# RWKV-7 recurrence and a squared-ReLU feed-forward on one core: the first product for two chunks at a time, the second in whole tiles

## The chip, the core and the metric

One core of a Trainium2 chip. The metric is the device time of one execution in microseconds. PE is TensorE with its matmuls (PEld its weight loads), DVE is VectorE, ACT is ScalarE, POOL is GpSimd, SP is SyncE, whose queue issues the loads and stores.

## What is computed

```python
def _attn_ref(r, k, v, w, a, b):        # each (4, 8, 768, 40), float32
    state = np.zeros((B, H, D, D))
    for t in range(S):
        y[:, :, t] = einsum('bhd,bhde->bhe', r_t, state)
        Sa = einsum('bhde,bhe->bhd', state, a_t)
        state = state * w_t[:, :, None, :] - Sa (x) b_t + v_t (x) k_t
    return y

def _moe_ref(x, w_in, w_out):           # x: 3072 x 320, w_in: 320 x 2048, w_out: 2048 x 320
    g = np.maximum(x @ w_in, 0.0) ** 2
    return g @ w_out

# x is y with the heads of a token side by side
```

## The kernel before

The sequence of 768 steps is cut into 12 chunks of 64 tokens. A chunk holds 64 tokens of 4 batches, 256 tokens in all. For each chunk c the work is:

- `load`: SP issues the loads of w, k, b, a, v, r (`ldw` ... `ldr`), 320 KB each, into buffers that alternate between two chunks.
- `prep`: ln of w (ACT), its split into two bf16 parts `hi` and `lo`, cumulative sums by matmuls (`ci`, `cx`, `cg`), their exponentials (`ei`, `ex`, `eg` on ACT), the scaled k and b (`mulKB`), a (`mulA`), and casts of r and v; transposes on PE (`TK`, `TA`) with their evictions (`tK`, `tA`, `tR`).
- `rec`: the masked products `EN` (masked by `mEN` on DVE, line 542), then `AS`, `EV`, `u0`, `NU`, `u1`, and the state `S`, `SC`, `s`, `TS`, `tS`. This goes from chunk to chunk.
- `read`: `TV`, `CX` (masked by `mCX`, line 542), `RS`, `Y`, `y`, `yd`, and the transposes `XT`, evicted by `xt` into the tile XT: the feed-forward's input, transposed.
- `ffn`: four operations `F c u0` to `F c u3` multiply XT by a quarter of w_in each into a PSUM slot; `f` (ACT, line 747) is the relu into the tile G, `q` squares G in place (DVE, line 753, or POOL, line 755); four operations `O c u0` to `O c u3` multiply G by w_out into one PSUM slot, `o` evicts it, `st` stores it.

PE's array is used in halves. F, the transposes, EN, CX and `ci` run as two half-arrays of 64 rows by 128 columns (mode "R"); O, EV, NU, S, Y, AS, RS, `cx`, `cg` as two of 128 rows by 64 columns (mode "C"). Consecutive matmuls alternate between the halves. One F is 20 matmuls with 256 columns each, one O is 16 with 320. There are four PSUM slots, each of 2 x 512 float32 a partition.

All operations are recorded in a `Plan` with their predecessors, but the order in which they are issued, the engine of each and the PSUM slot of each are written out by hand in the string ORDER, as entries "engine (slot) name". `Plan.issue` follows it: each engine gets its instructions in this order, and each waits for what it reads. Numbers such as `FETCH`, `SWITCH` or the durations in `plan.add` are notes from which such an order was made; at run time they do nothing. A helper records the matmuls (line 356 for products, 360 for transposes), so the lines of the profile name helpers and the tiles tell which operation it is.

An excerpt of ORDER, where PE's second form follows the first:

```
PE0 F 1 u0; POOL hi 4; ACT f 1 u3; DVE mulA 3; POOL wout1; PE1 F 0 u2; DVE lo 4; ACT f 1 u0;
DVE mulKB 3 h0; PE2 CX 2 g0; POOL mulKB 3 h1; PE3 CX 2 g1; ACT f 0 u2; PE0 F 1 u2
```

Of the kernel before, what the change touches and what calls it, by code (L numbers as in the profile page):

```python
# [23 lines left out]
class Plan:  # L24
# [6 lines left out]
    LINE, FETCH = 256, 3500  # L31
# [62 lines left out]
AS 1; DVE mEN 1 g1; PE1 TS 0; PE2 CX 0 g1; ACT tS 0; POOL win1; DVE mCX 0 g1; PE EV 1; SP ldv 2;
PE0 CX 0 g0; ACT u0 1 g1; DVE mCX 0 g0; ACT u0 1 g0; POOL mulKB 2 h1; PE NU 1; DVE mulKB 2 h0; PE1
Y 0; ACT u1 1 g0; PE2 TK 2; DVE y 0; ACT u1 1 g1; SP ldw 3; DVE mulA 2; ACT tK 2; PE0 TV 1; POOL
castR 2; PE1 S 1; DVE yd 0; POOL win0; PE SC 1; DVE tV 1; SP lda 3; PE3 XT 0; PE2 TA 2; ACT xt 0;
DVE s 1 q1; PE0 CX 1 g0; ACT tR 2 g1; DVE s 1 q0; PE3 F 0 u3; ACT tA 2; DVE mCX 1 g0; PE1 TS 1;
POOL castV 2; ACT tR 2 g0; DVE tS 1; PE0 CX 1 g1; ACT f 0 u3; PE2 F 0 u1; SP ldw 4; DVE mCX 1 g1;
ACT ln 3; PE1 EN 2 g0; PE3 EN 2 g1; ACT f 0 u1; POOL hi 3; DVE mEN 2 g0; PE0 RS 1; PE Y 1; SP ldb  # L100
3; POOL lo 3; PE2 AS 2; DVE mEN 2 g1; PE1 F 0 u0; DVE y 1; POOL win2; SP ldk 3; PE EV 2; ACT f 0
u0; PE3 cx 3; DVE yd 1; DVE u0 2 g1; PE0 ci 3 h1; ACT u0 2 g0; PE cg 3; POOL q 0 u1; ACT ei 3 h1;
PE NU 2; ACT eg 3; PE1 ci 3 h0; DVE u1 2 g0; ACT u1 2 g1; PE0 XT 1; ACT ln 4; DVE xt 1; PE2 S 2;
POOL q 0 u0; PE SC 2; ACT ei 3 h0; SP ldr 3; PE0 TV 2; DVE s 2 q0; ACT ex 3; PE1 F 1 u1; DVE tV 2;
POOL wout0; PE3 F 1 u3; ACT f 1 u1; DVE s 2 q1; PE0 F 1 u0; POOL hi 4; ACT f 1 u3; DVE mulA 3;
POOL wout1; PE1 F 0 u2; DVE lo 4; ACT f 1 u0; DVE mulKB 3 h0; PE2 CX 2 g0; POOL mulKB 3 h1; PE3 CX
2 g1; ACT f 0 u2; PE0 F 1 u2; DVE mCX 2 g1; PE1 cx 4; ACT f 1 u2; POOL castR 3; DVE mCX 2 g0; PE
cg 4; POOL wout2; SP ldr 5; PE3 TK 3; ACT ex 4; PE0 ci 4 h0; POOL q 0 u2; DVE tK 3; PE2 TA 3; ACT
eg 4; PE1 RS 2; ACT tR 3 g0; PE Y 2; DVE tA 3; SP ldv 3; ACT tR 3 g1; PE3 O 0 u0; POOL wout3; ACT
ei 4 h0; DVE y 2; SP ldw 5; PE2 EN 3 g0; DVE yd 2; PE O 0 u1; DVE mEN 3 g0; PE0 EN 3 g1; POOL q 1  # L110
u0; PE1 ci 4 h1; DVE mEN 3 g1; PE2 XT 2; ACT ei 4 h1; PE O 0 u2; DVE q 1 u1; POOL q 0 u3; PE1 AS
3; PE0 O 1 u0; SP ldk 4; DVE zu 3; ACT castV 3; DVE q 1 u2; PE O 1 u1; DVE q 1 u3; ACT xt 2; SP
ldb 4; PE EV 3; PE O 1 u2; DVE u0 3 g1; ACT u0 3 g0; PE O 0 u3; PE NU 3; DVE o 0; ACT ln 5; PE O 1
u3; ACT u1 3 g1; DVE u1 3 g0; POOL hi 5; SP st 0; PE2 TS 2; SP lda 4; ACT o 1; POOL zu 4; DVE lo
5; PE3 TV 3; ACT tS 2; PE1 F 2 u1; SP ldr 4; DVE tV 3; POOL castR 5; PE0 F 2 u0; ACT f 2 u1; DVE
mulKB 4 h0; PE2 CX 3 g0; SP ldk 5; PE3 F 2 u3; ACT f 2 u0; POOL q 2 u1; DVE mCX 3 g0; SP lda 5;
PE1 CX 3 g1; PE0 ci 5 h0; ACT f 2 u3; DVE mulKB 4 h1; PE2 F 2 u2; POOL q 2 u0; DVE mCX 3 g1; ACT
ei 5 h0; SP ldb 5; PE3 cx 5; ACT f 2 u2; PE0 RS 3; DVE q 2 u3; PE cg 5; POOL castR 4; PE Y 3; ACT
ex 5; DVE mulA 4; PE1 ci 5 h1; POOL q 2 u2; SP ldv 4; PE2 TK 4; ACT eg 5; DVE y 3; ACT ei 5 h1;
PE3 TA 4; PE1 S 3; DVE tK 4; ACT tA 4; PE SC 3; POOL yd 3; SP ldw 6; PE0 O 2 u0; ACT tR 4 g0; DVE  # L120
s 3 q0; POOL mulA 5; ACT tR 4 g1; PE2 EN 4 g1; PE O 2 u1; DVE mEN 4 g1; SP ldr 6; PE3 XT 3; DVE s
3 q1; POOL mulKB 5 h0; PE2 EN 4 g0; ACT xt 3; PE O 2 u2; DVE mulKB 5 h1; SP st 1; DVE mEN 4 g0;
PE1 TA 5; POOL castV 4; PE3 TK 5; ACT tR 5 g0; PE O 2 u3; DVE tK 5; ACT tR 5 g1; PE2 AS 4; ACT o
2; PE EV 4; DVE tA 5; PE3 TS 3; ACT u0 4 g0; SP st 2; DVE u0 4 g1; PE0 F 3 u1; SP ldw 7; ACT ln 6;
DVE tS 3; SP ldv 5; POOL hi 6; PE NU 4; ACT f 3 u1; PE1 EN 5 g0; DVE u1 4 g0; PE3 F 3 u0; POOL lo
6; SP ldr 7; DVE u1 4 g1; PE0 F 3 u3; ACT f 3 u0; DVE mEN 5 g0; POOL zu 5; SP ldk 6; PE2 ci 6 h1;
ACT f 3 u3; PE3 TV 4; POOL q 3 u0; PE1 S 4; SP ldb 6; DVE tV 4; ACT ei 6 h1; PE SC 4; PE0 cx 6; PE
cg 6; DVE s 4 q0; POOL q 3 u1; PE2 CX 4 g0; ACT ex 6; SP ldb 7; PE3 F 3 u2; DVE s 4 q1; ACT eg 6;
ACT castR 6; DVE mCX 4 g0; PE0 EN 5 g1; PE1 O 3 u0; ACT f 3 u2; SP lda 6; DVE mEN 5 g1; ACT castV
5; POOL q 3 u2; PE2 CX 4 g1; PE3 ci 6 h0; PE O 3 u1; DVE q 3 u3; ACT ei 6 h0; SP ldw 8; DVE mCX 4  # L130
g1; PE0 AS 5; ACT ln 7; PE3 RS 4; PE O 3 u2; POOL hi 7; DVE mulKB 6 h0; PE Y 4; POOL lo 7; PE EV
5; DVE y 4; PE O 3 u3; ACT u0 5 g0; DVE u0 5 g1; POOL yd 4; ACT o 3; DVE mulKB 6 h1; PE NU 5; POOL
mulA 6; PE2 ci 7 h0; SP st 3; ACT u1 5 g0; DVE u1 5 g1; PE3 XT 4; PE1 TK 6; SP ldr 8; ACT ei 7 h0;
DVE xt 4; PE0 TS 4; SP lda 7; ACT tK 6; POOL zu 6; PE2 TV 5; DVE tS 4; SP ldv 6; PE3 F 4 u0; DVE
tV 5; POOL castR 7; PE0 TA 6; ACT f 4 u0; SP ldk 7; PE1 F 4 u1; DVE tR 6 g0; ACT tR 6 g1; POOL q 4
u0; DVE tA 6; PE2 CX 5 g1; PE3 F 4 u2; ACT f 4 u1; DVE mCX 5 g1; SP ldv 7; PE0 EN 6 g0; PE1 F 4
u3; ACT f 4 u2; POOL q 4 u1; DVE mEN 6 g0; PE2 CX 5 g0; SP ldw 9; ACT f 4 u3; PE3 S 5; DVE mCX 5
g0; PE SC 5; POOL castV 6; PE0 EN 6 g1; ACT ln 8; PE1 ci 7 h1; DVE mEN 6 g1; PE2 O 4 u0; ACT ei 7
h1; SP ldb 8; POOL q 4 u2; DVE s 5 q1; PE1 RS 5; PE0 cx 7; PE cg 7; DVE s 5 q0; PE Y 5; ACT ex 7;
DVE mulKB 7 h1; PE3 AS 6; POOL hi 8; PE EV 6; ACT castR 8; DVE mulA 7; PE O 4 u1; POOL zu 7; ACT  # L140
u0 6 g0; DVE y 5; PE O 4 u2; ACT eg 7; ACT u0 6 g1; POOL q 4 u3; DVE mulKB 7 h0; PE NU 6; DVE yd
# [700 lines left out]
```

## Time and profile before

| | us |
|---|---|
| median of 3 runs | 269.33 (268.33 to 271.39) |
| the profiled execution, time | 270.12 |
| its span, first to last instruction | 268.4 |
| PE busy in it | 226.9 (85%) |
| DVE busy | 198.1 (74%) |
| ACT busy | 160.1 (60%) |
| POOL busy | 141.5 (53%) |

The granted TensorE clock was 0.975 of full speed on average. Busy time of an engine is the union of its instructions. In the profile's groups a line reads: line, engine, operation, out<-in with shapes, count, then busy time and mean ns of one, then the idle time of the engine just before them and what ended it. "issue" as releaser means that the engine waited for nothing the profile shows. The queues of part 3 are those of the DMA engines; q8 carries instructions.

### The profile page before, as it was taken

How to read it: one execution, taken by the hardware profiler on the slowest of the kernel's cores; microseconds unless marked ns; L12 is line 12 of the kernel's file. 1: busy time of each engine (PE TensorE's matmuls, PEld its weight loads, DVE VectorE, ACT ScalarE, POOL GpSimd, SP SyncE). 2: the span in 40 equal slices, each digit the busy share in tenths (PEclk: the TensorE clock that was granted, in tenths of full speed). 3: DMA queues.
4: the chain of work that ended last, by engine and by line, in shares of the span. 5: the costliest groups of instructions: out<-in, count | busy, mean ns of one | idle time of the engine just before them, and what ended most of it. 6: DMA issues, size and time to landing. Idle time of an engine off the chain costs nothing.

```text
span 268.4 us, 14323 instructions
## 1 busy us (share of the span) xinstructions
PE 226.9 (85%) x6712; PEld 193.6 (72%) x6712; DVE 198.1 (74%) x219; ACT 160.1 (60%) x201; POOL 141.5 (53%) x119
## 2 busy tenths in 40 slices
PE   0557884987979998997998898997879999999992
PEld 0335774776869986876888786886767888878881
DVE  7456578495886797996789898894888697867620
ACT  3346565636735774674674784775756877674631
POOL 4384634086570686674599287793483293232020
PEclk9999999597999999999799999999999999999999
DMA  7999999975993579799898298799980410200213
GB/s 116 185 185 143 153 193 149 136 127 58 171 171 56 114 142 142 180 169 153 181 155 116 53 145 155 133 124 171 158 165 8 89 19 2 54 5 2 51 26 74
DMA packets 135995, 31.06 MB, mean 116 GB/s; under 512 B 125185, under 2 KB 135937, under 8 KB 135937
## 3 DMA queue, kind: packets, MB, share of 16 engines
q1 hardware_dynamic: 131136, 27.53, 62.8%
q0 software_dynamic: 4800, 2.62, 7.7%
q8 instruction: 52, 0.85, 1.4%
q14 instruction: 7, 0.05, 0.1%
HBM read 28.84 MB, written 3.93 MB: 122 GB/s over the span
## 4 chain that ended last, share of the span: by engine, by line
PE 63%; DVE 13%; issue 7%; ACT 5%; DMA 5%; SPq 4%; POOL 3%; ACTq 0%; POOLq 0%; DVEq 0%
PE pb L356 55%; PE pb L360 8%; DMA raw_kb<-in_k_dram 2%; DVE KB L352 2%; DMA raw_r<-in_r_dram 2%; POOL lo L350 1%; ACT VU L342 1%; DVE EN L542 1%; DVE Yb L337 1%; DVE VU L339 1%; SPq L385 1%; SPq L778 1%; POOL tR L346 1%; DVE Yb L702 1%; ACT VUT L342 1%
## 5 line engine op out<-in xcount | busy, mean ns | idle before, releaser
L755 POOL TENSOR_TENSOR G<-G 128x1024 bf16<-128x1024 bf16 x30 | 57.6, 1929 | 53.0 <-ACT G L747 52.6
L356 PE MATMUL pb<-WOUT,G 128*64 128x320 bf16 x768 | 59.4, 300 | 3.8 <-issue 3.7
L747 ACT ACTIVATE G<-pb 128x1024 bf16<-128x1024 f32 x48 | 49.0, 1024 | 22.2 <-PE pb L356 21.1
L356 PE MATMUL pb<-XT,WIN 64*128 64x256 bf16 x960 | 60.8, 273 | 1.0 <-issue 0.9
L356 PEld LDWEIGHTS <-WIN 64*128 64x128 bf16 x960 | 46.9, 96 | 6.4 <-issue 1.7
L356 PEld LDWEIGHTS <-G 128*64 128x64 bf16 x768 | 42.9, 110 | 11.4 <-issue 5.5
L542 DVE TENSOR_TENSOR EN<-pb,MSK 128x1024 bf16<-128x1024 f32 x24 | 29.1, 1221 | 6.3 <-PE pb L356 6.0
L542 DVE TENSOR_TENSOR CX<-pb,MSK 128x1024 bf16<-128x1024 f32 x24 | 29.0, 1218 | 4.4 <-PE pb L356 4.2
L346 POOL CAST hi<-lnW 128x640 bf16<-128x640 f32 x11 | 8.6, 779 | 37.1 <-ACT lnW L409 17.9
L431 ACT ACTIVATE iG<-pb 128x640 f32<-128x640 f32 x24 | 16.8, 702 | 11.3 <-PE pb L356 10.6
L352 DVE TENSOR_TENSOR KB<-raw_kb,iG 128x640 bf16<-128x640 f32 x17 | 18.8, 1113 | 6.2 <-ACT iG L431 3.7
L356 PEld LDWEIGHTS <-EN 128*64 128x64 bf16 x768 | 16.4, 118 | 7.4 <-issue 5.3
L342 ACT ACTIVATE NZ<-pb 64x640 bf16<-64x640 f32 x19 | 13.2, 697 | 13.6 <-PE pb L356 9.0
L634 DVE TENSOR_TENSOR STb<-pb,gL 64x640 bf16<-64x640 f32 x22 | 18.1, 821 | 4.2 <-PE pb L356 3.7
L342 ACT ACTIVATE AR<-pb 128x512 bf16<-128x512 bf16 (+1 forms) x24 | 15.5, 667 | 8.3 <-PE pb L360 5.4
L753 DVE TENSOR_TENSOR G<-G 128x1024 bf16<-128x1024 bf16 x18 | 17.5, 979 | 3.0 <-ACT G L747 3.0
L342 ACT ACTIVATE VU<-pb 64x640 bf16<-64x640 f32 x15 | 10.5, 698 | 9.8 <-PE pb L356 7.3
L339 DVE TENSOR_SCALAR VU<-pb 64x640 bf16<-64x640 f32 x9 | 7.4, 823 | 10.0 <-ACT VU L342 6.2
L350 POOL TENSOR_TENSOR KB<-raw_kb,iG 128x640 bf16<-128x640 f32 x7 | 11.4, 1628 | 5.8 <-DMA raw_kb<-in_k_dram 3.6
L356 PE MATMUL pb<-hi,UTI 64*128 64x320 bf16 x48 | 8.6, 342 | 7.0 <-POOL hi L346 6.9
L342 ACT ACTIVATE osb<-pb 128x640 f32<-128x640 f32 x11 | 7.8, 705 | 11.2 <-PE pb L356 11.1
L350 POOL TENSOR_TENSOR lo<-lnW,hi 128x640 bf16<-128x640 f32 x8 | 13.0, 1622 | 2.4 <-PE pb L360 2.0
(88 smaller groups left out, 454.3 us busy)
## 6 DMA issues: line engine op xcount, KB each, us to landing
raw_w<-in_w_dram SPq DMA_DIRECT2D x24, 160.0 KB, 5.0
raw_kb<-in_k_dram SPq DMA_DIRECT2D x12, 320.0 KB, 6.1
raw_r<-in_r_dram SPq DMA_DIRECT2D x24, 160.0 KB, 4.1
raw_kb<-in_b_dram SPq DMA_DIRECT2D x12, 320.0 KB, 6.7
raw_a<-in_a_dram SPq DMA_DIRECT2D x24, 160.0 KB, 5.2
raw_v<-in_v_dram SPq DMA_DIRECT2D x12, 320.0 KB, 6.6
out_dram<-osb SPq DMA_DIRECT2D x24, 160.0 KB, 2.7
WIN<-in_moe_w_in_dram POOLq DMA_DIRECT2D x8, 160.0 KB, 4.6
```

Source lines behind the costliest of these rows:

```text
L342: alts.append(("ACT", c_act(n), lambda: nc.scalar.activation(out=o_(), in_=i_(), func=ACTF.Copy, scale=1.0 if scale is None else scale)))
L346: lambda: nc.gpsimd.tensor_copy(out=o_(), in_=i_())))
L350: return [("POOL", 130 + 2.35 * n, lambda: nc.gpsimd.tensor_tensor(out=o_(), in0=a_(), in1=b_(), op=op)), ("DVE", c_dve(n), lambda: nc.vec ...
L352: ("DVE", c_dve(n), lambda: nc.vector.tensor_tensor(out=o_(), in0=a_(), in1=b_(), op=op))]
L356: return lambda: nc.tensor.matmul(out=o_(), lhsT=l_(), rhs=r_(), start=start, stop=stop, skip_group_check=True)
L360: return lambda: nc.tensor.transpose(out=o_(), in_=i_(), identity=IDb[rows(g), :])
L431: ew(f"ei {c} h{jh}", [("ACT", c_act(2 * n), lambda hb=hb, jh=jh: nc.scalar.activation(out=iG[0][:].rearrange("p (g j) e -> p g (j e)", g= ...
L542: evac(f"m{nm} {c} g{g}", lambda s, n: [("DVE", c_dve(n), lambda: nc.vector.tensor_tensor(out=dst[q2][:, g, s].rearrange("p q i t -> p (q ...
L634: ew(f"s {c} q{q}", [("DVE", c_dve(2 * n), lambda q=q: nc.vector.tensor_tensor(out=STb[q2][rows(q), :, q, 0:D], in0=slot(hs, FP32)[rows(q) ...
L747: ("ACT", c_act(1024), lambda gb=gb, hf=hf: nc.scalar.activation(out=gb, in_=slot(hf, FP32)[:], func=ACTF.Relu)),
L753: ("DVE", 165 + 0.7 * 1024, lambda gv=gv: nc.vector.tensor_tensor(out=gv, in0=gv, in1=gv, op=ALU.mult)),
L755: ("POOL", 1900, lambda gv=gv: nc.gpsimd.tensor_tensor(out=gv, in0=gv, in1=gv, op=ALU.mult))],
```

## The change

Chunks are put in groups: chunk 0 alone, then pairs (1, 2) to (9, 10), chunk 11 alone. For a group of two, F runs with 512 columns, both chunks side by side in XT; one F operation then covers one block of 128 columns of w_in in each half (`v0`, `v1`) and fills the same PSUM slot, with 10 matmuls. O stays per chunk, but in whole tiles: 128 rows by 128 columns (mode "D"), 8 matmuls instead of 16 an operation. G holds a whole group and there is one of it instead of two for a chunk each. The two buffers of v lie in the lower and upper 64 partitions of one tile. ORDER is a new one: the same 911 entries in number, in another sequence and with other choices of engine (f three times on DVE; q 24 times on each of DVE and POOL instead of 18 and 30; mulKB 13 times on POOL instead of 7). Its notes on load and fetch durations are changed too.

```diff
-    LINE, FETCH = 256, 3500
+    LINE, FETCH = 256, 4350
...
+GROUPS = ((0,), (1, 2), (3, 4), (5, 6), (7, 8), (9, 10), (11,))
+NGB = 1
-ORDER = """SP ldw 0; SP ldk 0; SP ldw 1; SP ldr 0; ACT ln 0; POOL hi 0; SP ldb 0; POOL zu 2; DVE lo 0; SP lda
+ORDER = """DVE zu 0; SP ldw 0; SP lda 0; SP ldr 0; SP ldb 0; ACT ln 0; SP ldw 1; POOL hi 0; POOL zu 1; SP ldk
+0; POOL lo 0; ACT castR 0; PE0 cx 0; PE1 ci 0 h0; SP ldr 1; PE2 ci 0 h1; PE cg 0; SP ldv 0; ACT ln
...
+AS 5; PE EV 5; DVE tA 6; PE3 F 4 u0v0; DVE tR 6 g0; ACT u0 5 g0; DVE u0 5 g1; PE0 F 4 u3v1; SP ldk
+7; ACT f 4 u0v0; DVE mulKB 6 h1; POOL mulKB 6 h0; PE NU 5; DVE f 4 u3v1; PE3 cx 7; ACT u1 5 g1; PE
+cg 7; POOL q 4 u0v0; SP ldw 8; ACT ei 7 h0; DVE u1 5 g0; PE0 TK 6; ACT ex 7; PE1 ci 7 h1; DVE tK
...
+g0; PE2 F 4 u3v0; DVE tS 4; POOL q 4 u1v1; DVE mCX 5 g0; PE0 TS 5; SP lda 7; ACT f 4 u3v0; PE3 F 4
+u1v0; DVE tS 5; SP ldw 9; POOL q 4 u0v1; ACT ln 8; PE1 EN 6 g1; PE2 CX 5 g1; ACT f 4 u1v0; PE0 F 4
+u2v1; DVE mEN 6 g1; PE3 TK 7; POOL hi 8; DVE mCX 5 g1; ACT f 4 u2v1; PE1 AS 6; PE EV 6; POOL lo 8;
+ACT castR 7; DVE tK 7; PE0 O 3 u0; ACT u0 6 g0; SP ldr 9; POOL q 4 u2v1; DVE q 4 u1v0; PE2 ci 8
...
-    raw_v = buf("raw_v", [64, NH, D], FP32, NV)
+    raw_v = buf("raw_v", [128, NH, D], FP32)[0]
...
-    XT = buf("XT", [128, NKB, NT], BF16, 2)
-    G = buf("G", [128, NFB, NT], BF16, 2)
+    XT = buf("XT", [128, NKB, 2 * NT], BF16, 2)
+    G = buf("G", [128, NFB, 2 * NT], BF16, NGB)
...
-                 nc.sync.dma_start(out=raw_v[c % NV][:], in_=whole(v))}),
+                 nc.sync.dma_start(out=raw_v[rows(c % NV)], in_=whole(v))}),
...
+    def up(gi):
+
+        gr = GROUPS[gi]
+        c, w = gr[-1], NT * len(gr)
+        gb = G[gi % NGB]
+        xt = XT[gi % 2]
+        per = 512 // w
+        for u in range(4):
+            for v_ in range(2 // per):
+                hf = ("F", c, u, v_)
+                us = f"u{u}" + (f"v{v_}" if per == 1 else "")
+                blk = range(v_ * per, v_ * per + per)
+                ms = []
+                for i in blk:
+                    for kb_ in range(NKB):
+                        for rg in range(2):
+                            ms.append(mm(
+                                lambda rg=rg, i=i, hf=hf: slot(hf, FP32)[
+                                    :, rg, w * (i % per):w * (i % per) + w],
+                                lambda rg=rg, kb_=kb_, i=i, u=u: WIN[
+                                    rows(rg), kb_, 256 * u + 128 * i:256 * u + 128 * i + 128],
+                                lambda rg=rg, kb_=kb_: xt[rows(rg), kb_, 0:w],
+                                i == blk[0] and kb_ == 0, kb_ == NKB - 1))
+                pe(f"F {c} {us}", "R", w, ms,
+                   reads=[("XT", gi % 2, ci) for ci in range(len(gr))] + [("WIN", u)],
+                   writes=[hf], alloc=[hf])
...
+        for c in gr:
+            down(c, gi, gr.index(c))
+
+    def down(c, gi, ci):
...
             for j in range(4 * u, 4 * u + 4):
                 for g in range(2):
-                    for bb in range(2):
-                        ms.append(mm(
-                            lambda g=g, bb=bb: slot(ho, FP32)[rows(bb), g, 0:DM],
-                            lambda g=g, bb=bb, j=j: G[q2][
-                                :, j, (2 * g + bb) * L:(2 * g + bb) * L + L],
-                            lambda j=j: WOUT[:, j, :], j == 0, j == NFB - 1))
+                    ms.append(mm(
+                        lambda g=g: slot(ho, FP32)[:, g, 0:DM],
+                        lambda g=g, j=j: G[gi % NGB][
+                            :, j, NT * ci + 2 * g * L:NT * ci + 2 * g * L + 2 * L],
+                        lambda j=j: WOUT[:, j, :], j == 0, j == NFB - 1))
...
-        ffn(c)
+        for gi, gr in enumerate(GROUPS):
+            if gr[-1] == c:
+                up(gi)
```

In the names of F, f and q of a pair, the chunk is the pair's second: F 2 is the product of chunks 1 and 2. The eviction `f` and the square `q` still take 1024 elements a row, and there are as many of each as before.

## The prediction

> **What bounds the kernel now.** I read the page's first and third part and its groups, then the timeline of PE, the waits and the windows; behind these I numbered the 6712 matmuls of the trace in order of start and matched them with the fixed order, so that every operation has a duration "first matmul to first matmul of the next".
>
> ```profile
> PE 226.9 (85%) x6712; PEld 193.6 (72%) x6712; DVE 198.1 (74%) x219; ACT 160.1 (60%) x201; POOL 141.5 (53%) x119
> ...
> q8 instruction: 52, 0.85, 1.4%
> ...
> L755 POOL TENSOR_TENSOR G<-G 128x1024 bf16<-128x1024 bf16 x30 | 57.6, 1929 | 53.0 <-ACT G L747 52.6
> L356 PE MATMUL pb<-WOUT,G 128*64 128x320 bf16 x768 | 59.4, 300 | 3.8 <-issue 3.7
> ...
> L356 PE MATMUL pb<-XT,WIN 64*128 64x256 bf16 x960 | 60.8, 273 | 1.0 <-issue 0.9
> ...
> L356 PEld LDWEIGHTS <-G 128*64 128x64 bf16 x768 | 42.9, 110 | 11.4 <-issue 5.5
> ```
>
> PE is the fullest engine, and F and O (the two products) are half of its work. The fourth thing to see is small: queue q8 brings 52 transfers, 0.85 MB, of instructions. PE has 13,424 instructions (a load and a matmul each time); 0.85 MB over these is 64 B each, so one 16 KB transfer is 256 instructions, or 128 matmuls.
>
> ```profile
> 156.06 0.17 PE L356 MATMUL pb<-SEL,hi 128*64 128x2 bf16 x2
> 156.09 0.17 PE L356 MATMUL pb<-SEL,lo 128*64 128x2 bf16 x2
> 156.20 0.41 PE L356 MATMUL pb<-AR,KBT 64*128 64x64 bf16 x16
> 156.44 1.26 PE L356 MATMUL pb<-XT,WIN 64*128 64x256 bf16 x20
> 157.54 0.40 PE L356 MATMUL pb<-AR,VUT 64*128 64x64 bf16 x16
> ```
>
> ```profile
> 160.46 1.26 PE L356 MATMUL pb<-WOUT,G 128*64 128x320 bf16 x16
> 161.55 0.45 PE L356 MATMUL pb<-STb,AR 128*64 128x80 bf16 x16
> 161.83 0.66 PE L356 MATMUL pb<-VU,EN 128*64 128x40 bf16 x32
> 162.34 0.30 PE L356 MATMUL pb<-WOUT,G 128*64 128x320 bf16 x1
> 163.92 0.87 PE L356 MATMUL pb<-WOUT,G 128*64 128x320 bf16 x10 [1.28 <-issue]
> ```
>
> Columns: start, duration, matmuls merged. From start to start, an F (20 matmuls) takes 1.10 us (median of all 1.092), an O (16) 1.09 (1.087), a 32-matmul operation with 40 or 64 columns 0.47 to 0.51. Starts within one form follow after 0.03 us; where the array's form changes (128*64 to 64*128 at 156.09) after 0.11 to 0.12: a change of form costs 0.09 to 0.10 us. And in the last two lines PE stops for 1.6 us inside one O whose inputs are there: "issue".
>
> ```profile
> PE pb L356 <- issue: 11.4, 11, 2.9
> ```
>
> Where do such stops lie? Of those inside an operation, 13 stand at matmuls 734, 990, 1502, 2142, 2653, 3293, 3933, 4445, 4573, 4701, 4829, 4957 and 5725: each is 94 plus a multiple of 128 (one is off by one). So they are ends of instruction blocks, 15.3 us in all, and a transfer of q8 ends 1.3 to 1.8 us before PE goes on. Between the stopped end and the block's beginning lie 4.1 to 5.0 us while the inputs stream (median 4.5; once 5.7, at 47 us), and 3.3 after they are loaded. I take 4.4 and 3.4: a block can't be shorter, whatever is in it. The switch between the two is at 200 us:
>
> ```profile
> 180.00:200.00 20.00, 16.56 (x585) 14.94 (x579) 14.95 (x16) 12.44 (x17) 12.18 (x9) 1.00 0.90 155
> 200.00:220.00 20.00, 19.34 (x619) 16.15 (x619) 16.15 (x18) 13.34 (x18) 9.65 (x8) 1.00 0.27 50
> ```
>
> (second last column: share of the DMA engines.) The Trainium skill says the opposite in "Runtime: NRT & Kernel Launch", section Instruction fetch mechanics: the fetch of the next page runs beside the current one and is mostly hidden. The trace disagrees by those 15.3 us.
>
> **The sum of before, block by block.** For each block I added the undisturbed durations of its operations and 0.095 us for each change of form. All blocks: 202.2 us. Blocks 0 to 11 end at 77.8 us and hold only 36.5 us of work: there inputs and elementwise work limit. Blocks 12 to 38 hold 105.0 us and took 122.8; the larger of work and 4.4 us, added up, is 122.5. Blocks 39 to 51 hold 54.6 and took 56.3 (with 3.4 us: 55.5). The rest: 6.1 to the last matmul, 5.5 for eviction and store. 77.8 + 122.8 + 56.3 + 6.1 + 5.5 = 268.5, the span. So after 78 us nearly all loss is blocks that hold only small operations and last less than their successor's fetch.
>
> **The change, part by part.**
>
> F with 512 columns. From 256 columns at 109.2 ns a pair and 320 at 135.9: 64 columns are 26.7 ns, so a pair costs columns/2.4 + 2.5 ns, and 512 columns 216 ns. Ten matmuls are 1.08 us against 1.09: 52.4 becomes 52.0 us. Gone are 400 matmuls and as many loads.
>
> O in whole tiles: 8 matmuls for 16. Whole tiles don't occur in the trace. If the load hides, each is 320/2.4 + 2.5 = 136 ns, again 1.09 us. If it doesn't, the bounds are 29 ns (a half's load and stream together, in the 0.466 us of 32 transposes) and 110 ns (the LDWEIGHTS row): 384 of them, +11 to +42 us. I take zero: today each half takes its next weights while its own stream runs, or a pair could not be within 2.5 ns of streaming, and in an O both halves use all 128 rows. The Trainium skill ("TensorE: Matmul & The Clock Gate", Part 3) says that a load overlaps with matmuls in flight only where the row group differs; the O rows here contradict it. By that rule the time is that of the fourth rival.
>
> Changes of form: counted in the two orders, 97 before and 132 after, 61 of them with whole tiles. 35 x 0.095 = +3.3 us (0 to twice that if whole tiles drain differently). PE's work is 205.1 us, +2.9.
>
> Instruction blocks: 784 matmuls less, 5928 in all, 47 blocks for 53. This is the gain. With the new order, blocks 12 to 36 (the last load stands in block 36) hold 115.3 us; 11 are under 4.4 us, against 20 of 27 before; the larger of both adds up to 126.4. Blocks 37 to 45: 49.4, with 3.4 us 49.6. Loss 11.3 us against 18.3. With 4.1 or 4.8 us it would be 123.3 or 131.4.
>
> The start. Blocks 0 to 11 hold 33.6 us and nearly no F: the order does the recurrence up to EN 3 before the second group. Before, EN 3 was through at 80.5 us, with F 0, F 1 and part of O 0 done. The loads up to it are the same 25. In SP's queue k of chunk 0 moves from second to sixth, so the first KB comes some 2 us later, but half of it goes to POOL (1.63 beside 1.11 us instead of 2.2 in a row) and castR 0 to ACT, which held TA 0 until 17.9. Block 0 should end as before, near 17.7. Eleven blocks at 4.7 (the mean of the stopped ones before 78 us) give 69.3; adding the 7.5 us which the same count leaves for data waits in blocks 1 to 11 of before gives 76.8. I take 75, nearer the second: up to there DVE has about 50 us of work.
>
> One buffer G. The relu of a pair waits for the last O of the pair before. In the new order the O of a pair all stand ahead of the next pair's F, so this costs nothing while the squares are done in time: between F 4 u0v0 and O 3 u3, PE has 22.9 us of listed work, POOL 17.7 (six squares at 1.93, 6.1 else). A late POOL is covered up to about 4 us; beyond that O waits, behind it all PE work, then f on ACT.
>
> Elementwise work by rows: DVE 197.3 to 203.5, ACT 164.6 to 158.7, POOL 141.2 to 135.1, nothing at its limit; the three f on DVE and the second half of raw_v (castV from the upper 64 rows) I cost as their rows, 1.2 us each. Every load keeps its bytes and its two buffers.
>
> Sum: 75 + 126.4 + 49.6 + 6.7 (last block) + 5.5, and 1.2 for what the same formula lacked before (0.3 and 0.8), = 264.4 us of span. The profiled execution is 268.4 of span and 270.12 of time, 0.8 above the median, 269.33. Change -4.0; forecast 265.3.
>
> **Rivals.**
> 1. The stalls are replaced, not removed: with PE fuller, waits for DVE and POOL take the place, and the loss after block 12 stays 19.5 us. Then +7: 272.3. For it: DVE has 131 us of work between EV 3 and EV 11, 87% of my time for that stretch, against 83% before. Against it: before, that loss fits blocks to 0.3 us. The skill's page on fetching would give this too.
> 2. The single G buffer, the slower side. Place: O of each pair, waiting for squares on POOL. From 4 us of lateness on, each further us is one on PE, five pairs: at 3 us, 15: 280. For it: POOL is full for 17.7 of those 22.9 us, and twice as much work hangs on one pair. Against: the 4 us of cover, and that before the squares had POOL waiting for the relu (52.6 us), not the other way.
> 3. The start runs at the fetch alone (69.3) and blocks take 4.1: 264.4 - 5.7 - 3.1, plus 0.9: 256.5. Against it: DVE would be over 85% busy from 22 us on.
> 4. Loads of whole tiles aren't hidden: 276 to 307.
>
> **How the numbers follow.** Forecast 0.45 (own range 259 to 269), rivals 0.22, 0.13, 0.13, 0.07. The range 256 to 280 leaves out the fourth and the ends of the second and third. A measurement here can tell about 1% from no change, that is 266.6 to 272.0. Faster: 0.35 of the forecast's share and all of the third, 0.48. Same: 0.08 of the forecast and 0.09 of the first, 0.17. Slower: 0.35, from the first's upper part, 2, 4, and 0.02 of the forecast.
>
> **What would show it.** F from start to start 1.08 for ten matmuls, O 1.09 for eight; if O takes 1.3 or more, rival 4. q8: 46 transfers. "Issue" stops of PE fewer, at multiples of 128 matmuls. Block 12 begins near 75 us. PE waiting on G by POOL would show rival 2. I am wrong if the block ends don't stop PE although blocks are short, or if EN 3 is later than 80 us.

## The result and the profile after: 283.5 us, 5.5% slower

| | before | after |
|---|---|---|
| median of 4 runs each | 268.83 us (267.15 to 271.39) | 283.54 us (280.55 to 284.21) |
| ratio after / before | | 1.0548 (95% interval 1.0437 to 1.0659) |
| span of the profiled execution | 268.4 us | 282.5 us |
| PE's chain share / DVE's | 63% / 13% | 58% / 23% |

The forecast was 265.3 us with a range of 256 to 280. The span alone came out 18.1 us above the sum of 264.4. Later comparisons ran on other chips, where the kernel before took 271.3 to 272.6 us; across them only ratios to the kernel before of the same batch are compared. Ratios and their 95% intervals use the runs in the fast state alone; the profiled executions of b_defer, a_lkb and a_lqkb were slow ones (clock 0.920, 0.897 and 0.908), so of these three the totals are read from the ratios.

First the lines that answer to those shown of before: part 1, the instruction queue and the groups of the two products in the page of the kernel after.

```profile
PE 236.0 (84%) x5928; PEld 170.1 (60%) x5928; DVE 204.8 (72%) x227; ACT 153.9 (54%) x196; POOL 136.7 (48%) x116
...
q8 instruction: 46, 0.75, 1.2%
...
L362 PE MATMUL pb<-WOUT,G 128*128 128x320 bf16 x384 | 59.6, 307 | 0.8 <-DVE G L772 0.8
L362 PE MATMUL pb<-XT,WIN 64*128 64x512 bf16 (+1 forms) x560 | 58.7, 351 | 0.8 <-DVE VU L345 0.5
```

The instructions fell as planned (5928 matmuls, 46 transfers), and the two products take what they took. PE's busy share is no higher (84% for 85%) and the span is 14 us longer: most of that time went into waits. The waits of PE in the kernel after (columns: total us, times, longest):

```profile
PE pb L366 <- issue: 3.6, 3, 2.3
PE pb L362 <- issue: 3.2, 4, 1.8
PE pb L362 <- DVE EN L548: 2.9, 4, 1.2
PE pb L366 <- DVE KB L358: 2.5, 1, 2.5
```

"Issue" fell from 11.4 us on the product line to 3.2, while on the transposes (L366) it rose from 1.3 us to 3.6. What took its place are many waits for DVE, the longest of them 2.5 us. The chain that ended last, in the page of before and then of after, says the same in one line each:

```profile
PE 63%; DVE 13%; issue 7%; ACT 5%; DMA 5%; SPq 4%; POOL 3%; ACTq 0%; POOLq 0%; DVEq 0%
```

```profile
PE 58%; DVE 23%; ACT 6%; issue 6%; SPq 3%; DMA 3%; POOL 0%; ACTq 0%; DVEq 0%
```

To place the loss I matched every matmul with its operation, as in the prediction, and gave each its undisturbed duration plus 0.095 us for a change of form. What is left over is a stop at a block end (matmul 94 + 128 n, inside an operation), another gap of more than 0.2 us ("wait"), or matmuls that run slower than undisturbed. Sums in us:

| kernel | first matmul | work | block ends | waits | slower | last matmul | span |
|---|---|---|---|---|---|---|---|
| before | 6.9 | 202.1 | 15.4 | 22.1 | 16.4 | 262.9 | 268.4 |
| after | 7.3 | 204.9 | 8.6 | 35.9 | 20.3 | 277.0 | 282.5 |

and the work that PE did in each stretch:

| us | 0-40 | 40-80 | 80-120 | 120-160 | 160-200 | 200-240 |
|---|---|---|---|---|---|---|
| before: work | 12.7 | 26.0 | 37.1 | 33.0 | 32.7 | 37.8 |
| after: work | 11.1 | 22.3 | 28.9 | 35.3 | 34.1 | 36.5 |
| before: waits | 13.6 | 3.1 | 0.6 | 3.4 | 0.7 | 0.7 |
| after: waits | 15.7 | 8.9 | 5.2 | 2.4 | 0.9 | 2.8 |

In work done, PE is 5.3 us behind at 80 us and 13.5 us behind at 120 us, and at 240 us still 11.1. So the loss is made by 120 us. The windows 80 to 120 us of before and of after show how the engines stood (columns: window, length, busy us of PE, PEld, DVE, ACT and POOL with instruction counts, granted clock, share of the DMA engines, GB/s):

```profile
80.00:120.00 40.00, 38.34 (x1144) 33.41 (x1138) 33.49 (x36) 26.09 (x34) 22.91 (x17) 1.00 0.73 133
```

```profile
80.00:120.00 40.00, 33.41 (x721) 21.78 (x717) 27.77 (x27) 20.21 (x25) 22.68 (x15) 0.92 1.01 159
```

All engines were busy for less of this time, except POOL and the DMA engines. The timeline of the kernel after shows what such a stretch is made of; first DVE, then POOL:

```profile
103.00 1.03 DVE L772 TENSOR_TENSOR G<-G 128x1024 bf16<-128x1024 bf16 x1
...
106.55 2.13 DVE L772 TENSOR_TENSOR G<-G 128x1024 bf16<-128x1024 bf16 x1
108.61 2.34 DVE L548 TENSOR_TENSOR EN<-pb,MSK 128x1024 bf16<-128x1024 f32 x2
110.87 1.96 DVE L772 TENSOR_TENSOR G<-G 128x1024 bf16<-128x1024 bf16 x1
112.76 1.82 DVE L343 CAST hi<-lnW 128x640 bf16<-128x640 f32 x1
114.68 1.97 DVE L358 TENSOR_TENSOR lo<-lnW,hi 128x640 bf16<-128x640 f32 x1
```

```profile
106.24 6.04 POOL L774 TENSOR_TENSOR G<-G 128x1024 bf16<-128x1024 bf16 x3
112.25 3.72 POOL L356 TENSOR_TENSOR KB<-raw_kb,iG 128x640 bf16<-128x640 f32 x2
115.93 2.12 POOL L356 TENSOR_TENSOR tA<-raw_a,Gex 128x640 bf16<-128x640 f32 x1
```

```profile
116.71 0.44 PE L362 MATMUL pb<-lo,UTX 128*64 128x320 bf16 x2 [1.75 <-DVE lo L358]
```

POOL multiplies without a break from 106 to 118 us, and the DVE operations that work in SBUF alone take about 2 us beside it (squares 2.13 and 1.96, against 1.03 at 103 us, where POOL's product ends in mid-square), while EN, which reads PSUM, keeps its time (2.34 us for two). The late `lo` then holds `cx 6` on PE for 1.75 us. The new order gives POOL 13 of the 24 products `mulKB` (21.9 us), the old one 7 (11.4 us).

### The profile page after: what moved, and what is told of

Read it like the earlier page. It is cut to its first block, busy times and chain, and to the rows that moved or that the text cites. A ratio compares the mean times of both kernels' runs of the same rounds, so it can differ in the third digit from the quotient of the medians.

```text
span 282.5 us, 12772 instructions
## 1 busy us (share of the span) xinstructions
PE 236.0 (84%) x5928; PEld 170.1 (60%) x5928; DVE 204.8 (72%) x227; ACT 153.9 (54%) x196; POOL 136.7 (48%) x116
## 4 chain that ended last, share of the span: by engine, by line
PE 58%; DVE 23%; ACT 6%; issue 6%; SPq 3%; DMA 3%; POOL 0%; ACTq 0%; DVEq 0%
PE pb L362 48%; PE pb L366 9%; DVE EN L548 4%; DVE tA L358 3%; DVE CX L548 2%; DVE G L772 2%; DVE VU L345 2%; DMA raw_w<-in_w_dram 2%; DVE KB L358 2%; DVE STb L640 1%; ACT VU L348 1%; SPq L381 1%; DVE lo L358 1%; DVE AR L343 1%; ACT AR L348 1%
## 5 line engine op out<-in xcount | busy, mean ns | idle before, releaser
L774 POOL TENSOR_TENSOR G<-G 128x1024 bf16<-128x1024 bf16 x24 | 47.4, 1988 | 58.5 <-ACT G L764 58.5
L362 PE MATMUL pb<-WOUT,G 128*128 128x320 bf16 x384 | 59.6, 307 | 0.8 <-DVE G L772 0.8
L362 PE MATMUL pb<-XT,WIN 64*128 64x512 bf16 (+1 forms) x560 | 58.7, 351 | 0.8 <-DVE VU L345 0.5
L362 PEld LDWEIGHTS <-G 128*128 128x128 bf16 x384 | 35.7, 100 | 17.9 <-issue 1.5
L362 PEld LDWEIGHTS <-WIN 64*128 64x128 bf16 x560 | 27.5, 96 | 20.1 <-issue 2.3
L772 DVE TENSOR_TENSOR G<-G 128x1024 bf16<-128x1024 bf16 x24 | 24.3, 1023 | 5.0 <-ACT G L764 4.9
L356 POOL TENSOR_TENSOR KB<-raw_kb,iG 128x640 bf16<-128x640 f32 x13 | 21.9, 1688 | 8.8 <-ACT iG L437 5.4
L348 ACT ACTIVATE AR<-pb 128x512 bf16<-128x512 bf16 (+1 forms) x23 | 15.1, 670 | 13.6 <-PE pb L366 7.8
L640 DVE TENSOR_TENSOR STb<-pb,gL 64x640 bf16<-64x640 f32 x22 | 18.1, 821 | 4.9 <-PE pb L362 4.6
L362 PE MATMUL pb<-hi,UTX 128*64 128x320 bf16 x48 | 8.8, 367 | 8.9 <-POOL hi L352 7.3
L362 PEld LDWEIGHTS <-UTX 128*64 128x64 bf16 x96 | 5.5, 126 | 14.9 <-issue 9.7
L343 DVE COPY KBT<-pb 128x2048 bf16<-128x2048 bf16 x10 | 12.2, 1218 | 3.0 <-PE pb L366 2.9
L366 PE MATMUL pb<-IDb,KB 64*128 64x64 bf16 x384 | 9.8, 205 | 4.6 <-DVE KB L358 2.5
```

The costliest lines, as they stand in the source:

```text
L348: alts.append(("ACT", c_act(n), lambda: nc.scalar.activation(out=o_(), in_=i_(), func=ACTF.Copy, scale=1.0 if scale is None else scale)))
L356: return [("POOL", 130 + 2.35 * n, lambda: nc.gpsimd.tensor_tensor(out=o_(), in0=a_(), in1=b_(), op=op)), ("DVE", c_dve(n), lambda: nc.vec ...
L362: return lambda: nc.tensor.matmul(out=o_(), lhsT=l_(), rhs=r_(), start=start, stop=stop, skip_group_check=True)
L366: return lambda: nc.tensor.transpose(out=o_(), in_=i_(), identity=IDb[rows(g), :])
L640: ew(f"s {c} q{q}", [("DVE", c_dve(2 * n), lambda q=q: nc.vector.tensor_tensor(out=STb[q2][rows(q), :, q, 0:D], in0=slot(hs, FP32)[rows(q) ...
L772: ("DVE", 165 + 0.7 * 1024, lambda gv=gv: nc.vector.tensor_tensor(out=gv, in0=gv, in1=gv, op=ALU.mult)),
```

## The experiments

Theories at the start: the order loses the time, or the forms do; and if it is the order, because PE's work is put off (D), or because DVE and POOL hold up the chain (P), or because of the loads.

**Which part: the new order with the old forms, singly and together.** order_only has the new order, groups and buffers, with 256-column F and O in halves; o_half undoes only the O form, f256 only the F form; b_o_whole is the old order with whole-tile O.

```diff
 # o_half, order_only (O in halves again)
-    ms.append(mm(lambda g=g: slot(ho, FP32)[:, g, 0:DM], ... 2 * L ...
+    for bb in range(2):
+        ms.append(mm(lambda g=g, bb=bb: slot(ho, FP32)[rows(bb), g, 0:DM], ... L ...
 # f256, order_only (one chunk at a time)
-    for i in blk:
+    for i, ci in [(i, ci) for i in blk for ci in range(len(gr))]:
```

> The new order with the old forms: F of a pair as 20 matmuls of 256 columns, O in two halves with 16 matmuls; pairs, one G and the order stay. Theory A (the new order loses the time: PE waits for elementwise work and inputs, and the forms are sound): block sums give 203.4 us of PE work (1.7 less, 110 changes of form) but 53 instruction blocks again and 7 us more of short blocks: 288, at any rate 283 or more. Theory B (512 columns and whole tiles themselves lose it): back to 268 to 271.

> The new kernel with O in two halves (16 matmuls), F with 512 columns. A: 202.9 us of work, 2.2 less, short blocks 3 us more: 284.5 (282 to 288). B, if whole tiles are at fault: 275 or less.

> The new kernel with F of a pair in 256-column matmuls, O in whole tiles. A: 205.5 us of work, short blocks 2 us more: 286 (283 to 289). B, if 512 columns are at fault: 277 or less.

> The old kernel and order with O in whole tiles alone (8 matmuls of 128*128 for 16). A: PE work 205.5 us (+3.3 for 35 more changes of form), 50 instruction blocks instead of 53, short blocks 6.4 us less: 266 (262 to 269). B: slower than 273.

Measured: order_only 281.31 us, ratio 1.0417 (1.0339 to 1.0495). f256 281.72, 1.0391 (1.0281 to 1.0500). o_half 280.46 (275.76 to 283.09), no interval. b_o_whole 271.15, 1.0020 (0.9967 to 1.0073). So the order loses the time, with either form. "The order" here includes the pairing of chunks and the single G, which all three keep; no run undoes those alone. In order_only the block-end stops fall to 9.6 us with no matmul saved, so most of that gain is the order's mixing, not the forms'. By the ratio on the first chip order_only and f256 are 280.0 and 279.3 us, 8 and 7 us below what was expected; o_half is 4 us below. All three lie outside their ranges, on theory A's side. b_o_whole missed its gain of 3 us: its stops fell only from 15.4 to 12.1 us, and its further changes of form took that back (work 205.4 us). In b_o_whole, too, whole tiles cost what the halves did:

```profile
L356 PE MATMUL pb<-WOUT,G 128*128 128x320 bf16 x384 | 58.9, 301 | 0.9 <-issue 0.8
```

**The loads left out.** a_nl and b_nl are after and before with the loads of chunks 2 to 11 not issued.

```diff
-                for g in range(2):
+                for g in range(2 if c < 2 else 0):
 ...                                  # likewise for every load
```

> The new kernel without the loads of chunks 2 to 11: each later chunk reads what chunks 0 and 1 left in the two buffers. If the input loads set the pace up to EV 3 (theory L), EV 3 comes at 70 us or earlier instead of 82 to 86, and the whole at 272 or less. If elementwise work sets it (theory E), EV 3 moves by less than 5 us and the whole stays above 276.

> The old kernel without the loads of chunks 2 to 11, as a measure for the new one. L: EV 3 at 72 or earlier instead of 84.9. E: EV 3 stays above 80; the whole loses only what the instruction fetch gains from free queues, 3 to 8 us.

Measured: a_nl 278.32 us, 1.0292 (1.0156 to 1.0428); b_nl 262.57, 0.9709 (0.9568 to 0.9851). Both get shorter by 2.6 to 2.9 points, so the difference between the kernels stays. EV 3 (the fourth chunk's step of the recurrence on PE, first matmul) comes at 82.4 and 83.4 us, against 85.7 and 84.9 with all loads: the loads do not hold the start. In b_nl every block-end stop is gone, 15.4 us to 0, with the same 52 transfers: there the stops were instruction transfers standing behind the loads. In a_nl 4.3 us of 8.6 are left; 3.6 of them lie between 69 and 81 us, where weights are still being loaded (DMA share 1.10 from 70 to 80 us), and one of 0.7 us at 191 us, where the share is 0.16, is not explained by loads. The Trainium skill ("Runtime: NRT & Kernel Launch", Instruction fetch mechanics) says that this fetch is mostly hidden; b_nl agrees with it, the kernels with their loads don't.

**POOL's squares cut.** a_lq and b_lq square only 64 of the 1024 elements of a row on POOL (128 in three of a_lq's squares). The expectations of b_lqkb and bd_lqkb below call this "64 of 256"; the edit is the same.

```diff
 # b_lq; a_lq cuts its differently shaped gv likewise
-    out=gv, in0=gv, in1=gv, op=ALU.mult))],
+    out=gv[:, 0:64], in0=gv[:, 0:64], in1=gv[:, 0:64], op=ALU.mult))],
```

> The new kernel with POOL's 24 squares on 64 columns a row instead of 1024 (the rest of these blocks stays unsquared): POOL is hardly busy with them and no longer runs beside DVE's SBUF operations. If DVE operations stretched by POOL cause the new waits (theory P), 274 or less, mulA and q on DVE near 0.81 and 0.68 us. If the new order just has too little PE work ready early (theory D), above 277.

> The old kernel with POOL's 30 squares on 64 columns instead of 1024. P: gains less than half of what the new kernel gains by the same edit. D: both gain about the same, 0 to 4 us here.

Measured: a_lq 276.48 us, 1.0224 (1.0079 to 1.0369), from 1.0548; b_lq 270.89, 1.0017 (0.9940 to 1.0094). The same cut is worth about three points in the one kernel and nothing in the other, and of the 5.5 points between the two orders 2.1 are left (give or take 1.6). The marks were 274 us for P and 277 for D: taken by the ratio on the first chip, a_lq is 274.9 us, nearer P. In a_lq PE's waits from 80 to 160 us fall from 7.6 to 2.8 us, and the same DVE operations are short; their lines in a_lq:

```profile
110.23 0.68 DVE L772 TENSOR_TENSOR G<-G 128x1024 bf16<-128x1024 bf16 x1
111.45 0.49 DVE L343 CAST hi<-lnW 128x640 bf16<-128x640 f32 x1 [0.54 <-PE pb L362]
112.05 0.83 DVE L358 TENSOR_TENSOR lo<-lnW,hi 128x640 bf16<-128x640 f32 x1
```

`lo` takes 0.83 us for 1.97, the square 0.68. The Trainium skill ("SBUF — State Buffer", Who interferes with whom) says that DVE and POOL share one pair of ports under an exclusive lock, that a DVE instruction with two inputs in SBUF needs it against a POOL instruction that reads SBUF, that a copy or cast can take it in a two-port mode, and that the later one blocks fully instead of sharing. These rows agree. In the kernel after, the POOL products beside which the two squares, `hi` and `lo` began end at 108.14, 112.28, 114.23 and 115.97 us; the DVE operations end 0.54, 0.55, 0.35 and 0.68 us later. That is 0.13 to 0.15 us less than each takes undisturbed in a_lq: this fits operations that stand still until POOL's instruction is over and then take their own time. POOL is held in turn: its product that began at 108.09 us, while the first square still ran, took 2.34 us against 1.89 for its neighbours.

**Work put off, in the old order.** b_defer is the kernel before with F 1, O 0 and O 1 and what hangs on them moved behind the recurrence steps EV 3 and NU 3.

```diff
-... PE1 F 1 u1; ... PE3 O 0 u0; ... PE0 O 1 u0; ... PE EV 3; ... DVE u1 3 g0; POOL hi 5; ...
+... PE EV 3; ... DVE u1 3 g0; PE3 F 1 u1; ... PE3 O 0 u0; ... PE O 1 u3; ... POOL hi 5; ...
```

> The kernel before with one edit of the order: the matmuls, casts, squares, copies and stores of F 1, O 0 and O 1 are moved behind 'u1 3 g0', so that PE has some 9 us less work behind it when EV 3 begins, as in the kernel after. Theory D (EV 3 comes at 82 to 86 us whatever PE has done, and what was put off is paid when PE is full): EV 3 still at 82 to 86 us, the whole 5 to 9 us longer, 274 to 278 us. Rival C (the time up to EV 3 is PE's own work, so putting off only swaps two stretches): EV 3 at 75 to 78 us and the whole within 2 us of before, 267 to 271.

Measured: 286.39 us, 1.0497 (1.0396 to 1.0599). EV 3 begins at 84.1 us. Here PE's timeline near EV 3 in before and then in b_defer; EV 3 and NU 3 are the VU,EN and NZ,EN lines:

```profile
82.69 2.42 PE L356 MATMUL pb<-WOUT,G 128*64 128x320 bf16 x32
84.91 0.69 PE L356 MATMUL pb<-VU,EN 128*64 128x40 bf16 x32
85.41 2.37 PE L356 MATMUL pb<-WOUT,G 128*64 128x320 bf16 x32
87.59 0.69 PE L356 MATMUL pb<-NZ,EN 128*64 128x40 bf16 x32
```

```profile
84.06 1.04 PE L356 MATMUL pb<-VU,EN 128*64 128x40 bf16 x32 [0.49 <-DVE VU L400]
86.76 1.05 PE L356 MATMUL pb<-NZ,EN 128*64 128x40 bf16 x32 [1.65 <-ACT NZ L342]
```

With 6.6 us less work done by 80 us, EV 3 comes 0.8 us earlier: the O between its steps had cost little, and without it PE waits for ACT. But the clock in b_defer was at half speed from 74.7 to 91.8 us (EV 3 takes 1.04 us for 0.69); by its undisturbed durations the matmuls between 75.8 us and EV 3 took some 2.5 us longer for it, and up to that much of a gain can be hidden here. The direction is theory D's; the loss, 13.5 us by the ratio, is more than its 5 to 9.

**Late work left out.** a_cut is the kernel after without 24 of the 32 matmuls of O 0 and of O 1.

```diff
-            for j in range(4 * u, 4 * u + 4):
+            for j in (range(4 * u, 4 * u + 4) if c > 1 else [15 if u == 3 else 4 * u]):
```

> The kernel after, with 24 of the 32 matmuls of O 0 and of O 1 left out (48 matmuls, 48 x 0.136 us = 6.5 us of PE's work, all of it put off behind EV 3; the output of chunks 0 and 1 is wrong by what they leave out). Theory D (from EV 3 on PE is full and pays for what was put off): 5 to 7 us shorter, 276.5 to 278.5 us. Rival P (from EV 3 to 160 us the chain through DVE and POOL sets the time, and PE's work there lies in its waits): within 2 us of after, 281.5 to 285.

Measured: 278.20 us; ratio 1.0214 (1.0066 to 1.0361), for 1.0548. That is 9 us by the ratios, give or take 5, so in D's direction and not clear of its 5 to 7. But the trace does not put it where D has it: from EV 3 to EV 4 pass 25.1 us (82.8 to 108.0) against 25.3 in after, and PE's waits from 80 to 120 us grow from 5.2 to 10.7 us. In that stretch the chain sets the pace, not PE's work. Of the 8.1 us between the two spans, 2.9 are there at EV 3 already (one cut O stands just ahead of it), and the rest comes later: behind EV 3 the block-end stops fall from 5.4 to 0.5 us. So D's "PE is full from EV 3 on" is wrong: it is full from about 120 us on.

**A fuller clock.** b_warm and a_warm put extra matmuls on zeros into PE's early waits (76 in a_warm; the kernel b_warm has 55, not the 49 that its text names).

```diff
+        pe(f"W {i}", "R", 512, [mm(... wz[:, 0:128] ..., wz[:], True, True)] * k_, ...)
-... PE3 TK 0; ... PE0 ci 1 h0; ...
+... PE3 W 1; PE3 TK 0; ... PE0 W 2; PE0 ci 1 h0; ...
```

> The kernel before with 49 extra matmuls of 512 columns on zeros, put into waits that PE has before 45 us, so that PE stands still less there. Theory K (the low granted clock early on sets when EV 3 comes): the granted clock is full some 10 us earlier than the 39.9 us of before, EV 3 at or below 80 us, the whole 3 to 6 us shorter, 263 to 266. Theory E (the chain through ACT, DVE and POOL sets EV 3, with matmuls a small part): EV 3 at 83 to 87 us whatever the clock, the whole within 2 us or up to 3 longer, since each extra matmul can hold up the next.

> The kernel after with 76 extra matmuls of 512 columns on zeros in PE's waits before 60 us. Theory K: the granted clock is full well before the 62 us of after, EV 3 at or below 80 us instead of 85.7, the whole 4 to 7 us shorter, 277 to 280. Theory E: EV 3 at 83 to 88 us, the whole within 3 us of after, 281 to 287.

Measured: b_warm 274.24 us, 1.0042 (1.0001 to 1.0084); a_warm 284.37, 1.0444 (1.0353 to 1.0535). The copy behind EV 3 comes at 90.3 and 90.0 us, against 85.6 and 86.6. a_warm's clock records are full from 16 to 50 us and at half speed for 17 us in all up to 67. The kernel after has no record before 62 us, and its matmuls run at about half rate until then (32 transposes in 0.83 us at 38 us, 0.46 at 64), although the profile's averages count such a stretch as full; a_lkb, in the same order, has half-speed records from 24 to 62. b_warm's records are no fuller between 40 and 71 us than those of before (17 us against 10 at half speed), and before 40 us the kernel before has none, so b_warm tests little. In a_warm a much fuller clock did not bring EV 3 forward: theory K gets no support for the kernel after, though the extra matmuls may have cost time there themselves.

**The load on DVE and POOL taken away.** In a_lkb and b_lkb all 24 `mulKB` run on 8 of the 40 columns of each head, 128 of 640 elements a row (the "64" of the expectations counts the padding of KB, which the product never covers); a_lqkb and b_lqkb cut POOL's squares too; o_lqkb does both to order_only, bd_lqkb to b_defer.

```diff
-    lambda part=part: part(KB[c % NK][:, :, 0:D]),
+    lambda part=part: part(KB[c % NK][:, :, 0:D])[:, :, :, 0:8],
 ...                                  # the same for raw_kb and iG
+    for x in KB:
+        nc.vector.memset(x[:], 0.0)
```

> The kernel before with the 24 products mulKB made on 8 of 64 columns of each head (the rest of KB stays zero, so the output is wrong by what they leave out): some 1.1 us less for each of the 17 on DVE and some 1.5 us for each of the 7 on POOL. Theory E (the time up to EV 3 is a chain through ACT, DVE and POOL that every chunk's mulKB lies in): the first copy behind EV 3 at 80 to 83 us instead of 85.6, the whole 2 to 5 us shorter, 264 to 267 us. Rival O (only the written order of PE's work sets the time): EV 3's copy within 1.5 us of 85.6, the whole within 2 us of before.

> The kernel after with the same 24 products on 8 of 64 columns (13 of them on POOL and 11 on DVE here). Theory E with P (DVE and POOL set the pace from the start to some 160 us and stretch each other): EV 3's copy at 80 to 84 us instead of 86.6, PE's work left at 120 us down from 142.6 us by 6 or more, the whole 7 to 11 us shorter, 272.5 to 276.5 us, so more than the kernel before gains from the same cut. Rival O: the whole within 2 us of after, 281.5 to 285.5.

> The kernel before with the products of the run above and also POOL's squares on 64 of 256 columns (the output is wrong by both). Theory E with P: as with the products alone, 263 to 267 us, since the squares alone brought nothing here. Rival O: within 2 us of before.

> The kernel after with both: mulKB on 8 of 64 columns and POOL's squares cut as in the run with the squares alone. Theory E with P: 267 to 272 us, so that of the 14 us between the kernels 4 to 6 are left over the kernel before with the same two cuts: what PE's order alone costs (put-off work, form changes). Rival O: 276 to 281, no better than the squares alone.

> The order of before with F 1, O 0 and O 1 put off behind 'u1 3 g0', and both cuts (mulKB on 8 of 64 columns, POOL's squares on 64 of 256; the output is wrong by both). Theory D (what is put off is paid whatever DVE and POOL have to do): the ratio to before 1.03 to 1.055, some 280 to 286 us, as far above the kernel before with the two cuts (1.004) as b_defer stood above before (1.050). Theory T (put-off work is paid because DVE and POOL, full from there on, cannot make good for it; with them light the backlog is worked off): 1.00 to 1.02, 270 to 276 us.

> The new order with the old forms (256 columns, half-arrays) and both cuts. Theory T: as the kernel after with both cuts, or 1 to 3 us better since 33 fewer form changes are made: ratio 1.00 to 1.012, 270 to 274.5 us, PE's work left at 120 us at 138 or below. Theory D: no better than 1.03, 279 us or more, with 139 to 141 us of work left at 120 us.

Measured, as ratios to before:

| order | full | squares cut | `mulKB` cut | both cut |
|---|---|---|---|---|
| before | 1 | 1.0017 (0.9940-1.0094) | 1.0218 (1.0114-1.0321) | 1.0038 (0.9978-1.0098) |
| after | 1.0548 (1.0437-1.0659) | 1.0224 (1.0079-1.0369) | 1.0287 (1.0176-1.0398) | 1.0113 (1.0021-1.0204) |
| new order, old forms | 1.0417 (1.0339-1.0495) | | | 1.0172 (1.0088-1.0256) |
| before with work put off | 1.0497 (1.0396-1.0599) | | | 1.0325 (1.0262-1.0387) |

The old order gains nothing from lighter squares, and nothing visible from lighter `mulKB`; with `mulKB` alone it even loses 2%, which is not explained. The second cut is not neutral, though: its memsets of KB stand ahead of `lo 0` on DVE in the old order (`lo 0` at 12.0 us for 7.9, EV 0 at 27.1 to 27.3 for 24.1), while in the new order `lo 0` is POOL's and EV 0 comes at 21.9 to 22.2 for 24.2. E's figures for the old order (264 to 267 and 263 to 267 us) were missed; by the ratio on the first chip a_lkb is 276.6 us, at the edge of its range, and a_lqkb 271.9, inside it. The new order gains 2.5 points in the old forms and 4.4 in the new. Measured against the old order with the same cuts, the new one loses 1.3 points (1.0172 - 1.0038, about 3.6 us, give or take 2.8) instead of 4.2, and the kernel after 0.8 (2 us, give or take 3) instead of 5.5. Up to 3 us of this closeness can be the memsets' delay of the old order; the squares alone, which need no memset, take the 5.5 points to 2.1. The chain turns back to PE; o_lqkb's page:

```profile
PE 73%; DVE 8%; ACT 6%; issue 6%; SPq 3%; DMA 2%; POOL 0%; ACTq 0%; DVEq 0%
```

and its window 80 to 120 us, where PE does 35.2 us of work for after's 28.9 and its waits are 1.9 us for 5.2:

```profile
80.00:120.00 40.00, 37.85 (x1084) 31.49 (x1082) 26.67 (x32) 25.91 (x33) 11.69 (x17) 0.97 0.93 152
```

bd_lqkb's 1.0325 is in D's range (1.03 to 1.055). It lies 2.9 points above b_lqkb (7.7 us): putting that much work off costs by itself, and with DVE and POOL loaded it costs 5.0 points. o_lqkb fell between the two expected figures (1.012 and 1.03), nearer the lower. Theory E's other half, that the products set EV 3, is not borne out: EV 3 begins at 85.1 to 86.0 us in a_lkb, a_lqkb and b_lqkb and at 90.5 in b_lkb. But in bd_lqkb EV 3 begins at 81.7, 4.1 us ahead of b_lqkb, with 4.4 us less work done by 80 us: with DVE and POOL light, EV 3 does follow PE's work, which b_defer did not show. So several limits lie close together there. Taken away alone, neither the loads, the products, PE's work (in the old order) nor the low clock (in the new one) brought EV 3 forward by more than 3.3 us, and by 2.9 us it moved in a_cut too, whose edit shortens one O ahead of it; no run shows what holds it at 82 to 90 us in every kernel.

## Why the prediction was wrong

**Right: the price of the forms.** F with 512 columns takes 1.08 us, O in whole tiles 1.09, a change of form the same 0.095, PE's work 204.9 us for 205.1 predicted, 46 transfers for 46. The fourth rival falls, and with it, for this form, the sentence of the Trainium skill's "TensorE: Matmul & The Clock Gate", Part 3, that a load overlaps with matmuls only where the row group differs: it would have shown these loads. (The same section also names a background weight buffer.)

**Right: the single G.** O waits 0.8 us for squares in all, and no relu `f` waits for an O: each of its waits ends with the F that it evicts. The second rival's mishap doesn't occur.

**Right in kind: the block ends.** They stop PE 8.6 us instead of 15.4. b_nl shows that they hang on the loads; order_only shows that the order would have cut them without the forms.

**Wrong: the start.** Block 12 was to begin at 75 us and began at 82.7; EV 3, 30 matmuls into it, was so to come at about 77 and came at 85.7. This is +7.7 us of the 18.1 missed. The step that failed is "Eleven blocks at 4.7 ... adding the 7.5 us which the same count leaves for data waits": it counted the start in PE's blocks, as if it went with the number of PE's instructions, and left out what holds PE there.

Block 0 already ended at 20.1 us instead of 17.7. The "1.63 beside 1.11" of the two halves of mulKB 0 did not happen: beside POOL's half (15.61 to 17.14 us) DVE's mulA 0 took 2.07 us for 0.81, and DVE's own half came only behind that, at 17.74 us.

Blocks 1 to 11 then took 62.6 us instead of 57.3. The part up to EN 3 is not what was late against before: EN 3 began at 78.0 and 78.2 us, for 78.8 and 80.4 before, and so within the sign of 80 us that the prediction set. But the chain up to there goes through DVE from 64.4 to 76.8 us almost without a break; the windows 60 to 80 us of before and of after (columns as above) show DVE busy for 18.1 of 20 us instead of 14.9, where the prediction had counted "about 50 us of work" for the whole start:

```profile
60.00:80.00 20.00, 16.79 (x492) 14.09 (x490) 14.90 (x16) 11.90 (x17) 13.21 (x11) 0.91 0.95 131
```

```profile
60.00:80.00 20.00, 16.52 (x542) 13.37 (x538) 18.10 (x21) 12.60 (x16) 11.84 (x15) 1.00 0.92 139
```

The masks of EN 3 are done at 80.8 us, and EV 3 still comes 4.9 us later. PE's timeline of the kernel after, just ahead of EV 3 (the last line):

```profile
82.69 0.32 PE L366 MATMUL pb<-IDb,Yb 64*128 64x64 bf16 x5 [2.29 <-issue]
82.94 2.32 PE L362 MATMUL pb<-WOUT,G 128*128 128x320 bf16 x8
85.19 0.74 PE L362 MATMUL pb<-STb,AR 128*64 128x80 bf16 x16
85.73 0.81 PE L362 MATMUL pb<-VU,EN 128*64 128x40 bf16 x32
```

A block end holds PE for 2.29 us, and the O behind it runs at half the clock (2.32 us for 1.09; a record of half speed stands at 82.7 to 86.1 us). These places are read from one trace; no run takes them away one by one. Nor does less work ahead of EV 3 bring it forward in full: in b_defer 6.6 us less moved it by 0.8 (with a low clock that can hide some 2.5), in bd_lqkb 4.4 us less by 4.1. Before, F 1, O 0 and O 1 had filled waits there for little; the prediction read their time as part of what delayed EV 3.

**Wrong: blocks 12 to 36.** Predicted 126.4 us, measured 136.1 with 115.3 of work, so a loss of 20.8 instead of 11.1. The failed step is the formula "the larger of work and 4.4", which has no term for waits, and the line "DVE 197.3 to 203.5 ... nothing at its limit". DVE's sum was right (204.8); the mistake was to judge it by its total. Between 99 and 117 us the chain ran from one DVE operation to the next, and those in SBUF were 2.4 to 3.7 times as long beside POOL. The first rival named this place, but its 272.3 us kept the predicted start and took the loss as unchanged at 19.5. Another +9.7 us; blocks 37 to 45 add 2.0 (51.6 for 49.6), the rest -1.3, together 18.1.

**What is shown and what isn't.** Shown by runs: the order (with its pairs and single G) and not the forms loses most of the time; putting work off costs by itself in the old order; most of the kernel after's loss goes when POOL's squares are made light (5.5 points to 2.1), and the old order gains nothing by that. How much of the rest lighter `mulKB` takes is blurred by its memsets. Only argued: how the loss of the uncut new order divides between the two, since they act together: less work is done while there is room, and then DVE and POOL leave PE hungry when it should catch up. Whether the forms add one point (1.0548 against 1.0417) is within the intervals.

## What to carry to other kernels

Work that fills a wait is free only where the wait is: before moving it later, ask whether the event behind the wait comes earlier at all, and price it in full if it doesn't. Judge an engine by the stretch where the chain runs through it and by what runs beside it, not by its sum over the span. A change in instruction form and a new order should be priced, and tried, apart.

## What the runs showed of the hardware

- Instruction transfers stop PE at the ends of 256-instruction blocks mainly while loads fill the queues: 15.4 us with them and 0 without in the old order, with the same 52 transfers; 8.6 and 4.3 us in the new one, 3.6 of the 4.3 while weights are loaded.
- DVE operations in SBUF beside a multiplying POOL: `lo` 0.83 to 1.97 us, a square 0.68 to 1.96, `hi`, a cast, 0.49 to 1.82; each ends 0.35 to 0.68 us behind POOL's instruction. POOL's own `mulKB` goes from 1.54 to 1.86 us (mean of two). An operation that reads PSUM keeps its time (two EN 2.34 us, 2.35 with a light POOL).
- Whole-tile matmuls with a new weight tile each time hide their loads: eight of 320 columns take 1.09 us. A change into or out of this form costs the same 0.095 us as between the half forms.
